# One list-scheduled program in place of phases: tiled attention matmuls with projections and MLP between them

## The chip, the cores and the metric

The kernel runs on one core of one Trainium2 chip. The metric is the time of one execution on the device, in microseconds (us). An execution also has a mean granted TensorE clock, where 1.00 is full speed. In the profile's lines PE is TensorE, PEld its weight loads, ACT ScalarE, DVE VectorE, POOL GpSimd, and PEclk the granted clock. On one core an execution is called slow here when it is over 1.5% longer than the fastest of the same kernel in the same comparison.

## The reference, cut to what matters

A gate mixes a 32-head attention with an MLP. S = 2048 rows, D = 640, head size 20, F = 1536, all in bfloat16.

```python
g = sigmoid((x * gate_w).sum(-1, keepdims=True))
q, k, v = heads(x @ wqkv)                     # 32 heads of 20
a = softmax(q @ k.T * 20**-0.5) @ v @ wo
h = x @ w1 + b1
b = (h * tanh(softplus(h))) @ w2              # Mish
out = g * a + (1 - g) * b
```

Two facts shape everything. A head of 20 fills only 20 of the 128 rows of TensorE in the score product, and 21 of its 128 columns (value plus a column of ones for the denominator) in the value product. And the exponentials are 32 x 2048 x 2048, that is 1.05 million columns of 128 partitions, all on ScalarE.

## The kernel before

First come the projections, the gate and the MLP; then a second block does all attention, then the output projection. In attention a step is one head, one tile of 128 keys and 1024 queries:

```python
def emit_S(s):
    ...
    for c in range(2):                     # KTZ: one head's keys, all other rows zero
        ins = pe.matmul(T[b][:, c * 512:(c + 1) * 512],
                        KTZ[j6][:, kt * P:(kt + 1) * P],     # 128 rows x 128 columns
                        QT[:, g6, q0:q0 + 512], start=True, stop=True)
    ins.then_inc(s_s, 1)

def emit_V(s):
    ...
    for c in range(2):                     # two matmuls on the same column tile
        ins = pe.matmul(OTACC[32 * j:32 * j + DH + 1, c * 512:(c + 1) * 512],
                        V_all[:, kt, h, 0:DH + 1], ETS[b][:, c * 512:(c + 1) * 512],
                        start=(kt == 0), stop=(kt == NKT - 1), tile_position=(0, 32 * j))
    ins.then_inc(s_v, 1)

for s in range(NS):
    emit_V(s)
    if s + ND < NS:
        emit_S(s + ND)
```

ScalarE does one exponential of 1024 columns per step, 1024 in all. No two matmuls share the array.

The softmax here doesn't subtract the row's maximum and nothing guards it: scores larger than these inputs give would overflow.

## Time and profile before

| | before |
|---|---|
| median of three executions | 1542.01 us (1541.35 to 1546.44) |
| projections, gate, MLP | about 365 us, PE 62%, ACT 49% |
| attention | 1109.5 us |
| normalisation of the last group, output projection, stores | about 59 us |
| mean granted clock | 0.955 |

The two lines below, of the page's list of costliest groups, give line, engine, operation, output and inputs, shapes, count, then busy time and mean ns of one, then idle time ahead of it and its releaser.

```profile
L499 ACT ACTIVATE ETS<-T 128x1024 bf16<-128x1024 f32 x1024 | 1048.7, 1024 | 69.3 <-PE T L558 23.8
L558 PE MATMUL T<-QT,KTZ 128*128 128x512 bf16 x2048 | 621.7, 385 | 4.9 <-DMA KTZ<-KT 4.9
```

In a matmul's line, 128\*128 is the part of the array in use, rows by columns. In attention the clock is 1.00 throughout; in the first part it goes down to a half around idle stretches of several us.

### The profile page before, as it was taken

To read this page: it belongs to the slowest core of one execution; us is meant where nothing else is said; L and a number is where in the kernel's file an instruction comes from. 1 tells how busy PE (TensorE), PEld (TensorE's weight loads), DVE (VectorE), ACT (ScalarE), POOL (GpSimd) and SP (SyncE) were. 2 spreads that over 40 slices of the span, in tenths; PEclk is the share of its full clock that TensorE was granted. 3 is DMA by queue.
4 is the path that set the end of the run, shared out by engine and by line. 5 is a ranking of instruction groups with operands and counts; after the bars stand their busy time and mean duration, and the time that the engine had idled before them with its cause. 6 is when DMAs were issued, how large, how long until landed. Compare 5 with 4: busy or idle time off the path is not lost.

```text
span 1541.6 us, 13886 instructions
## 1 busy us (share of the span) xinstructions
PE 1349.1 (88%) x5456; PEld 346.5 (22%) x5456; DVE 235.2 (15%) x200; ACT 1215.1 (79%) x1298; POOL 0.2 (0%) x4
## 2 busy tenths in 40 slices
PE   4665467557999999999999999999999999999958
PEld 2322223222212121121212121221212121121215
DVE  5211110012020202012020202012020202012027
ACT  0334536663999999999999999999999999999940
POOL 0000000000000000000000000000000000000000
PEclk9878779878999999999999999999999999999979
DMA  8000000001010101010110102010110101010011
GB/s 234 0 1 0 0 0 1 0 1 34 5 14 3 14 3 16 1 16 3 14 14 3 7 3 22 1 16 3 14 14 3 14 3 16 1 16 3 5 7 69
DMA packets 23753, 22.79 MB, mean 15 GB/s; under 512 B 14856, under 2 KB 19080, under 8 KB 23688
## 3 DMA queue, kind: packets, MB, share of 16 engines
q1 hardware_dynamic: 20584, 19.44, 9.8%
q10 hardware_dynamic: 3104, 2.46, 0.6%
q8 instruction: 43, 0.70, 0.2%
q14 instruction: 22, 0.18, 0.0%
HBM read 7.21 MB, written 2.62 MB: 6 GB/s over the span
## 4 chain that ended last, share of the span: by engine, by line
PE 73%; DVE 2%; DMA 0%; issue 0%; SPq 0%; ACT 0%; DVEq 0%
PE OTACC L575 35%; PE T L558 35%; PE T L592 2%; DVE OUNG L464 1%; DMA BCSB<-RTMP 0%; PE T L594 0%; DVE RTMP L468 0%; DVE KTZ L449 0%; SPq L538 0%; ACT ETS L499 0%; DVE OTACC L452 0%; DVE OUTT L487 0%; DVE DIFF L482 0%; DVE OTN L472 0%; DVEq L115 0%
## 5 line engine op out<-in xcount | busy, mean ns | idle before, releaser
L499 ACT ACTIVATE ETS<-T 128x1024 bf16<-128x1024 f32 x1024 | 1048.7, 1024 | 69.3 <-PE T L558 23.8
L575 PE MATMUL OTACC<-ETS,V_all 128*21 128x512 bf16 x2048 | 616.8, 383 | 15.1 <-DVE OUNG L464 13.1
L558 PE MATMUL T<-QT,KTZ 128*128 128x512 bf16 x2048 | 621.7, 385 | 4.9 <-DMA KTZ<-KT 4.9
L558 PEld LDWEIGHTS T<-QT,KTZ 128*128 128x128 bf16 x2048 | 116.8, 97 | 445.0 <-ACT ETS L499 429.5
L575 PEld LDWEIGHTS OTACC<-ETS,V_all 128*21 128x21 bf16 x2048 | 106.0, 90 | 451.5 <-issue 426.5
L464 DVE CAST OUNG<-OTACC 128x1024 bf16<-128x1024 f32 x16 | 19.6, 1225 | 834.7 <-PE OTACC L575 834.7
L300 PE MATMUL PB<-XT,WQKV 128*120 128x512 bf16 (+1 forms) x240 | 69.7, 427 | 81.7 <-DVE QT L345 81.7
L468 DVE RECIPROCAL RTMP<-OUNG 128x1024 bf16<-128x1024 bf16 x16 | 104.8, 6553 | 0.6
L316 PE MATMUL PB<-W,ACTT 128*128 128x512 bf16 x192 | 59.5, 408 | 35.0 <-ACT BALL L403 35.0
L394 ACT CAST KT<-PB 120x512 bf16<-120x512 f32 (+1 forms) x24 | 14.0, 585 | 95.6 <-PE PB L300 95.6
L286 PE MATMUL PB<-XT,W 128*128 128x512 bf16 x240 | 65.5, 424 | 11.2 <-ACT UB L370 10.8
L300 PEld LDWEIGHTS PB<-XT,WQKV 128*120 128x120 bf16 (+1 forms) x240 | 31.6, 142 | 116.2 <-DVE QT L345 93.0
L402 ACT CAST BALL<-PB 128x512 bf16<-128x512 f32 x16 | 9.3, 583 | 54.2 <-PE PB L318 54.2
L592 PE MATMUL T<-WOG,OTN 128*128 128x512 bf16 x128 | 36.3, 390 | 17.9 <-DVE OTN L472 17.9
L334 DVE TENSOR_TENSOR ACTT<-HB,UB 128x512 bf16<-128x512 bf16 x48 | 20.4, 425 | 171.9 <-ACT UB L380 168.3
L318 PE MATMUL PB<-W,ACTT 128*128 128x128 bf16 x192 | 44.0, 229 | 0.0
L234 PE MATMUL PB<-WQKV,XT 128*128 128x500 bf16 x80 | 23.7, 394 | 22.4 <-DMA XT<-in_A_x_dram 22.4
L286 PEld LDWEIGHTS PB<-XT,W 128*128 128x128 bf16 x240 | 25.2, 107 | 46.2 <-issue 13.6
L472 DVE TENSOR_TENSOR OTN<-OUNG,BCSB 128x1024 bf16<-128x1024 bf16 x16 | 11.1, 692 | 154.3 <-DMA BCSB<-RTMP 154.3
L316 PEld LDWEIGHTS PB<-W,ACTT 128*128 128x128 bf16 x192 | 19.9, 104 | 64.6 <-ACT BALL L403 38.1
L369 ACT ACTIVATE HB<-PB,B1F 128x512 bf16<-128x512 f32 x48 | 33.6, 700 | 0.7 <-PE PB L286 0.7
L370 ACT ACTIVATE UB<-PB,B1F 128x512 bf16<-128x512 f32 x48 | 33.9, 705 | 0.0
(36 smaller groups left out, 284.0 us busy)
## 6 DMA issues: line engine op xcount, KB each, us to landing
KTZ<-KT SPq DMA_DIRECT2D x64, 80.0 KB
BCSB<-RTMP SPq DMA_DIRECT2D x64, 64.0 KB, 5.9
W<-in_B_w_dram SPq DMA_DIRECT2D x2, 1920.0 KB, 12.9
out_dram<-OUTT SPq DMA_DIRECT2D x16, 160.0 KB, 1.8
WQKV<-in_A_wqkv_dram ACTq DMA_DIRECT2D x1, 2400.0 KB, 9.4
WOG<-in_A_wo_dram SPq DMA_DIRECT2D x4, 200.0 KB
B1T<-in_B_b_dram ACTq DMA_DIRECT2D x12, 0.2 KB, 8.4
XT<-in_A_x_dram SPq DMA_TRANSPOSE x5, 5.1
```

The costliest lines, as they stand in the source:

```text
L286: ins = pe.matmul(hp[:, 0:TCW], W1[:, ft, fc * P:(fc + 1) * P], XT[:, ft, tc * TCW:(tc + 1) * TCW], start=(ft == 0), stop=(ft == NFT - 1))
L300: ins = pe.matmul(QKP[0:mc, 0:512], WQKV[:, ft, c0:c0 + mc], XT[:, ft, qc * 512:(qc + 1) * 512], start=(ft == 0), stop=(ft == NFT - 1))
L316: pe.matmul(BPa[:, 0:512], ACTT[tc % 2][:, fc, tbl * P:(tbl + 1) * P], W2[:, fc, 0:512], start=(fc == 0), stop=(fc == NFC - 1))
L318: ins = pe.matmul(BPb[:, 0:128], ACTT[tc % 2][:, fc, tbl * P:(tbl + 1) * P], W2[:, fc, 512:640], start=(fc == 0), stop=(fc == NFC - 1))
L369: act.activation(HB[b][:, :], hp[:, 0:TCW], AF.Identity, bias=B1F[:, fc:fc + 1], scale=1.0)
L370: act.activation(UB[b][:, :], hp[:, 0:TCW], AF.Exp, bias=B1F[:, fc:fc + 1], scale=1.0).then_inc(s_hp_actdone, 1)
L464: ins = dve.tensor_copy(OUNG[:, :], OTACC[:, :])
L468: ins = dve.reciprocal(RTMP[:, :], OUNG[:, :])
L499: act.activation(ETS[b][:, :], T[b][:, :], AF.Exp, scale=SCALE).then_inc(s_e, 1)
L558: ins = pe.matmul(T[b][:, c * 512:(c + 1) * 512], KTZ[j6][:, kt * P:(kt + 1) * P], QT[:, g6, q0:q0 + 512], start=True, stop=True)
L575: ins = pe.matmul(OTACC[32 * j:32 * j + DH + 1, c * 512:(c + 1) * 512], V_all[:, kt, h, 0:DH + 1], ETS[b][:, c * 512:(c + 1) * 512], start ...
L592: pe.matmul(T[b][:, 0:512], OTN[:, g, atb * P:(atb + 1) * P], WOG[:, g, 0:512], start=(g == 0), stop=(g == NG - 1))
```

## The change

The intent: TensorE paces attention while ScalarE idles through the MLP, so let attention matmuls use several parts of the array at once and put all other matmuls into the time won. A planner runs on the host when the kernel is built. It simulates the five engines with assumed durations, picks the next operation of each engine by priority, and then writes five fixed instruction streams with the semaphores that they need. Below, a chunk is two or three score matmuls, a quad is four value matmuls, and a filler is a matmul of a projection, the MLP or the output projection put between them. The core of the diff:

```diff
+def s_cand(c):                       # a chunk of 3 or 2 units, in turn
+    ...
+        for i in range(n):
+            j = uu % 4
+            bank = (SA if c % 2 == 0 else SB_)[:, i * QW:(i + 1) * QW]
+            r = slice(32 * j, 32 * j + DH)             # row group j, 20 rows
+            ins = h.matmul(bank, KT[r, g, kt * P:(kt + 1) * P], QT[(qc * NG + g) % 3][r, :], start=True, stop=True)
+def v_cand(n):                       # a quad: four heads, four column groups
+    ...
+        for j in range(4):
+            ins = h.matmul(OT[32 * j:32 * j + DH + 1, :], V_all[:, kt, 4 * g + j, :], ETS[:, u % RU, :],
+                           start=(kt == 0), stop=(kt == NKT - 1))
+def e_cand(c):                       # exponentials of 1536 and 1024 columns
+    ...
+        return h.activation(ETS[:, a:a + n, :].rearrange("p u c -> p (u c)"), src, AF.Exp, scale=SCALE)
+def pick_pe():                       # scores first, then values, then a "fill":
+    ...                              # a matmul of a projection, the MLP or the output projection
-                act.activation(UB[b][:, :], hp[:, 0:TCW], AF.Exp, bias=B1F[:, fc:fc + 1],
...                                   # and Ln, Tanh, product
+                return h.activation(a, a, AF.Mish)     # 8 of 3072 columns, in two batches
```

Keys and queries of four heads lie at partitions 0, 32, 64 and 96, each padded by 12 rows of zeros. Evacuations of projections move from ScalarE to VectorE. Normalisation goes through three small transfers per group of four heads. The MLP is in two halves; the hidden layer of a half reuses the memory of weights that are done with.

## The prediction

> **What bounds the kernel now.** I read the strip of 40 slices first. It shows two programs one after the other:
>
> ```profile
> PE   4665467557999999999999999999999999999958
> ACT  0334536663999999999999999999999999999940
> PEclk9878779878999999999999999999999999999979
> ```
>
> Each slice is 38.5 us. For ten slices TensorE and ScalarE are both half busy and the clock is often lowered; then comes a long stretch in which both read 9; then a tail. A table of three stretches gives the sizes (columns: length, then busy time and count of PE, PEld, DVE, ACT, POOL, then granted clock, DMA share, GB/s):
>
> ```profile
> 25.00:365.00 340.00, 210.70 (x1096) 102.20 (x1094) 51.09 (x106) 165.08 (x273) 0.00 (x0) 0.83 0.03 10
> 373.00:1482.50 1109.50, 1096.09 (x4088) 221.94 (x4088) 129.32 (x47) 1045.87 (x1021) 0.00 (x0) 1.00 0.10 9
> 1482.50:1541.60 59.10, 36.98 (x258) 20.29 (x258) 35.81 (x35) 0.00 (x0) 0.00 (x0) 0.86 0.23 49
> ```
>
> So: about 365 us before attention, in which neither engine is full (PE 62%, ACT 49%); 1109.5 us of attention; 59 us of tail. In attention PE and ACT both look full, so the next question is which of them paces the other. The PE timeline of a few steps answers it (start, length, instruction, x how many merged):
>
> ```profile
> 800.09 0.60 PE L575 MATMUL OTACC<-ETS,V_all 128*21 128x512 bf16 x2
> 800.62 0.61 PE L558 MATMUL T<-QT,KTZ 128*128 128x512 bf16 x2
> 801.16 0.60 PE L575 MATMUL OTACC<-ETS,V_all 128*21 128x512 bf16 x2
> ```
>
> A pair of value matmuls and a pair of score matmuls start 0.535 us after each other, so a step is 1.07 us. In the same trace, columns stream at 0.42 ns each at full clock (late output projection: 640 columns each 0.27 us), so 512 columns take 0.216 us and a pair 0.43; about 0.10 us is lost each time PE changes between the two kinds. 4 x 0.216 + 2 x 0.10 = 1.07: PE explains the step alone. ACT's own pace I take from four activations in a row that wait for nobody:
>
> ```profile
> 101.72 2.19 ACT L380 ACTIVATE UB<-UB 128x512 bf16<-128x512 bf16 x4
> L380 ACT ACTIVATE UB<-UB 128x512 bf16<-128x512 bf16 x48 | 26.3, 617 | 0.1
> ```
>
> Each lasts 0.617 us, yet four end in 2.19, so starts are (2.19 - 0.617)/3 = 0.524 apart: consecutive ones overlap by 0.093 us. An exponential of 1024 columns lasts 1.024 us and could therefore start every 0.931 us. It does not:
>
> ```profile
> 796.99 11.72 ACT L499 ACTIVATE ETS<-T 128x1024 bf16<-128x1024 f32 x11
> ```
>
> (11.72 - 1.024)/10 = 1.07 us. **PE paces attention; ACT is 13% faster than it is used.** The chain of waits says the same: 35% of the span each for the two matmul lines, 0.1% for the exponential.
>
> **What the Trainium skill says.** "TensorE: Matmul & The Clock Gate", Part 3, gives for four row tiles of N=512 a measured gain of 3.07, for three column tiles 2.38. No concurrent tiles run in the kernel before: scores multiply a zero-padded 128-row operand, and consecutive value matmuls use the same column tile. So its trace can't confirm this, and the change hangs on it. "TensorEngine Tiling (Array Packing)", Key Properties, says that changing tiling mode drains TensorE; the 0.10 us at every change of kind agrees, though it may be partly the weight load behind the wait. "ScalarE: Activation LUTs", What ACT_TABLE_LOAD costs, gives 0.093 us of overlap between activations, as measured here, and 2.66 us for a change of table set; the load itself is 1.283 us in this trace. "DMA: Bandwidth & Descriptors" puts most of a transfer's fixed 2 us in its completion; the output stores here take 1.8 us from issue to landing.
>
> **The change part by part.**
>
> 1. *Phases merged.* Projections, the MLP and output projection become fillers between attention matmuls. The 365 us in front shrink to a start, and most of the 59 us tail goes.
>
> 2. *Scores on four row groups; values on four column groups.* A score chunk of 3 or 2 tiles goes to different row groups and banks, and a value quad to four column groups. From the gains above: a quad 4 x 0.216/3.07 = 0.28, three tiles 3 x 0.216/2.38 = 0.27, two some 0.25; plus 0.10 for the change of kind: 0.38, 0.37, 0.35 us. These are estimates.
>
> 3. *Exponentials of 1536 and 1024 columns in turn.* 32 heads x 16 key tiles x 4 query blocks = 2048 units of 512 columns; a pair of activations covers five, so 409.6 pairs. At ACT's own pace: 0.931 us for two units; for three, 512 columns more at 0.833 ns, 1.358 us. The pair is 2.289 us, and all of them 938 us. Before, the same columns took 1109.
>
> 4. *PE load beside this.* Each pair needs one chunk of three and one of two (0.72) and 1.25 quads (0.475): 1.20 us. Fillers in all: 560 matmuls of 512 columns (K 160, Q 160, first MLP layer 240) x 0.216 = 121; 640 of 320 columns x 0.135 = 86; 320 V matmuls of 160 columns, no faster than about 0.08 = 26. Sum 233 us, by 410 pairs 0.57. With one extra change per pair 0.1 to 0.2. Total 1.9 to 2.0 of the 2.289 us. **PE goes to some 85% and ACT becomes the bound.** The first quarter is denser: all of K and V, a quarter of Q and part of the first layer, some 80 to 100 us of fillers on 102 pairs, or 0.8 to 1.0 us a pair: with changes 2.2 to 2.4, at the limit.
>
> 5. *Mish in one activation instead of Exp, Ln, Tanh and copies.* The old MLP used 24 table loads. Now two batches of four activations of 3072 columns: 8 x (3072 x 0.833 ns + 0.17) = 22 us, plus four set changes x 2.66 = up to 11, less overlap: about 30 us, all on the ACT path. Evacuations go to DVE: some 200 at 0.5 to 0.7 us, with normalisation about 170 us, far from a bound.
>
> 6. *Start.* Before, PE waited 22.4 us for five 2048-row transposes. Now 512 rows come first (a quarter: issue in some 5 us instead of 18.8, plus 5.1 to land), then K and Q at half clock, 5 x 0.43 us each, and two evacuations: first exponential near 16 us, with some stalls before weights and later rows are in. I charge 24 us.
>
> 7. *Tail after the last exponential.* Quad and copy 1.1, three DMA hops of about 2, 2 and 3 us, reciprocal and multiply 1, eight output projections 64 x 0.135 = 9 us plus 2 for a cold clock, last evacuation and store 3: about 23 us.
>
> 8. *Stalls of ACT.* Dense first quarter about 10; after each Mish batch, in which no score can advance, PE cools and restarts at half clock: 2 x 4; at 32 group ends one accumulator bank is copied out before the next quad may start, about 0.5 each: 16. I charge 35 us.
>
> Sum: 938 + 30 + 24 + 23 + 35 = **1050 us**, 1.47 times faster.
>
> **Rivals.**
>
> *PE stays the bound because tiles do not overlap.* If score and value matmuls ran one after the other, they would need 4096 x 0.216 = 885 us plus changes, 1332 x 0.1 = 133, plus fillers 233: 1250, with start and tail about 1300. For it: PE is the bound today, and no tile runs concurrently in this trace. Against: operands lie at partitions 0, 32, 64, 96, outputs in separate banks or quadrants, issued in succession. Half the effect would put PE at 2.6 to 2.8 us a pair: about 1180.
>
> *The static order jams.* Every queue is fixed by a model with guessed durations (score chunk 0.226, 0.1 per change, a DMA 2.1). Where a DMA of the normalisation lands later than planned, DVE waits at its head with ready evacuations behind it, then PE, and ACT after two chunks. Per group 1 to 2 us would add 30 to 60: 1080 to 1110. For it: five queues in order and 1300 dependent steps. Against: the model's exponential pair is 2.232 us, slightly faster than I expect, so PE, DVE and DMA get a little more time than planned; output stores land in 1.8 us, within the 2.1.
>
> *The clock falls.* Shorter PE work leaves gaps. But in the old first phase the clock dropped around idle stretches of several us (95 to 105: no matmul, clock 0.64) and stood at 0.99 from 200 to 210 with 0.8 us gaps. Gaps here are below 1 us; a low clock doubles PE's work, which fills the gaps and lifts the clock again. Costs some 20 us if wrong.
>
> *Activations do not overlap* behind a semaphore wait: pairs at 1.024 + 1.451 = 2.475 us, 1014 in all, hence 1125 us.
>
> **Range and chances.** Everything as planned, with half the stalls, gives 1010 to 1020. Jams or lost overlap give 1080 to 1125. Range 1010 to 1120. Even without tile concurrency the merged phases save over 2%, so only a badly jammed order or an error I have not seen keeps it from being faster: 0.97 faster, 0.01 the same, 0.02 slower.
>
> **What would show it.** ACT at 9 from the second slice on, and mean exponential starts 2.29 us a pair in the middle; PE at 7 to 9 with score matmuls of a chunk starting together; clock 1.00 there; PE waiting on exponentials and ACT hardly on scores; the chain mostly on ACT; two Mish stretches of 13 to 15 us; first exponential before 20 us; 20 to 25 us after the last. The prediction is wrong if ACT waits for scores by more than some 50 us, if matmuls of one chunk start 0.2 us apart, or if DVE's waits on the broadcast transfers are copied by PE and ACT.

## The result

| | before | changed |
|---|---|---|
| median of all executions | 1543.01 us | 1124.43 us |
| executions | 1541.35 to 1546.44 | 1105.67, 1121.46 (fast), 1127.40, 1158.80 (slow) |
| mean clock of these | 0.955 (profiled) | 0.714, 0.698, 0.695, 0.662 |

The ratio of the fast executions is 0.7218 (0.7164 to 0.7272). Ratios are the mean time of one kernel's fast runs over that of the other's of the same rounds, so not quite the ratio of the medians. The result is correct.

The kernel is much faster, but its times are spread over 5% and are ordered exactly by the clock, which is far below that of before. These are three rows of the strip for the changed kernel, each slice 28 us:

```profile
PE   4999999998799988888999995999889988888785
ACT  2999999999866659999877999779998799999991
PEclk9999999999555575555556996559955555555556
```

For nine slices ACT is full and the clock is full. Then the clock falls to a half and, with two longer returns (72 and 58 us) and a few short ones, stays there; ACT has dips down to 5. A table of three stretches shows what a dip is (columns as in the prediction's table):

```profile
100.00:200.00 100.00, 94.85 (x661) 29.07 (x658) 29.59 (x47) 100.00 (x90) 0.00 (x0) 1.00 0.03 9
300.00:400.00 100.00, 100.00 (x475) 31.76 (x475) 13.03 (x25) 62.77 (x51) 0.00 (x0) 0.55 0.03 11
900.00:1000.00 100.00, 85.43 (x438) 15.71 (x435) 7.68 (x13) 94.92 (x84) 0.00 (x0) 0.50 0.03 9
```

From 100 to 200 us, with full clock, ACT is busy all the time although fillers are dense (661 matmuls). From 300 to 400 us PE is never idle, yet it gets through 475, and ACT through 51 exponentials instead of 90. From 900 to 1000 us there are few fillers, and even at half clock PE nearly keeps up. So a low clock hurts where fillers are dense.

The tiles do run together. This is the timeline at full clock, and after it one at half clock (weight loads and other engines' lines left out, but for one of ACT):

```profile
270.78 0.39 PE L487 MATMUL SA<-QT,KT 20*128 20x512 bf16 x3
271.10 0.40 PE L504 MATMUL OT<-ETS,V_all 128*21 128x512 bf16 x4
271.43 0.39 PE L408 MATMUL MB<-XT,W1F 128*128 128x512 bf16 x1
271.75 0.39 PE L487 MATMUL SB<-QT,KT 20*128 20x512 bf16 x2
```

```profile
331.30 0.61 PE L487 MATMUL SA<-QT,KT 20*128 20x512 bf16 x3
331.84 0.61 PE L504 MATMUL OT<-ETS,V_all 128*21 128x512 bf16 x4
331.95 1.45 ACT L583 ACTIVATE ETS<-SA 128x1536 bf16<-128x1536 f32 x1 [1.24 <-PE SA L487]
332.38 0.45 PE L422 MATMUL MB<-W,WKV 128*128 128x320 bf16 x1
332.76 0.61 PE L487 MATMUL SB<-QT,KT 20*128 20x512 bf16 x2
```

A chunk of three score tiles, a quad of four value tiles and one filler matmul each take 0.32 to 0.33 us from start to start, the change of kind included: three and four tiles cost what one matmul costs. At half clock the chunk and the quad take 0.54 (the filler there is a shorter one, of 320 columns), and ACT waits 1.24 us for the scores.

The groups of the exponentials, and the chain that ended last, of the changed kernel:

```profile
L583 ACT ACTIVATE ETS<-SA 128x1536 bf16<-128x1536 f32 x410 | 642.0, 1566 | 100.4 <-PE SA L487 99.5
L583 ACT ACTIVATE ETS<-SB 128x1024 bf16<-128x1024 f32 x409 | 465.7, 1139 | 16.3 <-PE SB L487 15.4
ACT 62%; PE 35%; DMA 1%; DVE 1%; SPq 1%; issue 0%
```

ACT waits 115 us for scores. The mean lengths, 1566 and 1139 ns, are not costs: one that waits for nobody lasts 1451 and 1024, and in a full queue the record is longer because consecutive ones overlap. Their starts tell the pace: the commonest distance is 1.347 us after an exponential of 1536 columns and 0.904 after one of 1024, 2.25 a pair.

With these, the 1119.7 us of the profiled execution add up. All four parts come from the starts and ends on ACT in the trace: the first exponential starts at 20.3; 410 x 1.347 + 409 x 0.904 = 922; the two Mish batches with their table loads take 13.3 each, 26.6; the last exponential ends 24.6 before the end. What is left, 126 us, is ACT waiting (the 115 us above, and the overlap that is lost at each wait).

### The profile page after: what moved, and what is told of

It reads as the page before. It is cut to its first block, busy times and chain, and to the rows that moved or that the text cites. A ratio compares the mean times of both kernels' runs of the same rounds, so it can differ in the third digit from the quotient of the medians.

```text
span 1119.7 us, 12597 instructions
## 1 busy us (share of the span) xinstructions
PE 981.2 (88%) x5616; PEld 262.8 (23%) x5616; DVE 191.2 (17%) x322; ACT 973.2 (87%) x833; POOL 8.9 (1%) x7
## 4 chain that ended last, share of the span: by engine, by line
ACT 62%; PE 35%; DMA 1%; DVE 1%; SPq 1%; issue 0%
ACT ETS L583 60%; PE MB L422 6%; PE OT L504 6%; PE SA L487 6%; PE MB L432 5%; PE SB L487 5%; PE MB L369 4%; PE MB L408 2%; ACT WKV L593 1%; ACT HHF L593 1%; DMA XT<-in_A_x_dram 1%; SPq L301 1%; PE MB L382 1%; DMA RB<-rdram 0%; DVE OTC L619 0%
## 5 line engine op out<-in xcount | busy, mean ns | idle before, releaser
L583 ACT ACTIVATE ETS<-SA 128x1536 bf16<-128x1536 f32 x410 | 642.0, 1566 | 100.4 <-PE SA L487 99.5
L583 ACT ACTIVATE ETS<-SB 128x1024 bf16<-128x1024 f32 x409 | 465.7, 1139 | 16.3 <-PE SB L487 15.4
L487 PE MATMUL SA<-QT,KT 20*128 20x512 bf16 x1230 | 212.2, 511 | 82.8 <-ACT ETS L583 69.2
L504 PE MATMUL OT<-ETS,V_all 128*21 128x512 bf16 x2048 | 265.2, 510 | 1.8 <-ACT ETS L583 1.0
L487 PE MATMUL SB<-QT,KT 20*128 20x512 bf16 x818 | 210.9, 510 | 15.9 <-ACT ETS L583 13.2
L408 PE MATMUL MB<-XT,W1F 128*128 128x512 bf16 x240 | 82.2, 416 | 0.0
L432 PE MATMUL MB<-WOG,OTN 128*128 128x320 bf16 x256 | 64.5, 395 | 10.0 <-DVE OTN L633 9.8
L369 PE MATMUL MB<-XT,WQP 128*128 128x512 bf16 x160 | 63.6, 483 | 0.0
L422 PE MATMUL MB<-W,WKV 128*128 128x320 bf16 x192 | 54.5, 399 | 9.7 <-ACT HHF L593 9.7
L422 PE MATMUL MB<-W,HHF 128*128 128x320 bf16 x192 | 55.0, 394 | 0.0
L619 DVE COPY OTC<-OT 128x512 f32<-128x512 f32 x32 | 22.1, 692 | 188.5 <-PE OT L504 188.4
L372 DVE CAST QT<-MB 128x512 bf16<-128x512 f32 x32 | 22.1, 691 | 147.9 <-PE MB L369 147.9
L633 DVE TENSOR_TENSOR OTN<-OTC,RB 128x512 bf16<-128x512 f32 x32 | 22.1, 691 | 105.4 <-DMA RB<-rdram 105.3
L432 PEld LDWEIGHTS MB<-WOG,OTN 128*128 128x128 bf16 x256 | 27.4, 117 | 43.5 <-issue 17.6
L385 DVE CAST KT<-MB 128x512 bf16<-128x512 f32 x32 | 22.1, 691 | 54.6 <-PE MB L382 54.6
L422 PEld LDWEIGHTS MB<-W,WKV 128*128 128x128 bf16 x192 | 19.4, 114 | 39.0 <-issue 19.2
```

Source lines behind the costliest of these rows:

```text
L369: return h.matmul(b[:, :], WQP[:, i, g * P:(g + 1) * P], XT[:, i, qc * 512:(qc + 1) * 512], start=(i == 0), stop=(i == NFT - 1))
L372: NFT, 216.0, lambda h, b: h.tensor_copy(QT[gi % 3][:, :], b[:, :]),
L385: lambda h, b: h.tensor_copy(KT[:, g, tc * 512:(tc + 1) * 512], b[:, :]), 600.0, [], ("K", g, tc))
L408: return h.matmul(b[:, :], W1[:, i, fc * P:(fc + 1) * P], XT[:, i, tc * 512:(tc + 1) * 512], start=(i == 0), stop=(i == NFT - 1))
L422: return h.matmul(b[:, 0:320], hslice(i, tl * P, P), W2[:, i, hh * 320:(hh + 1) * 320], start=(i == 0), stop=(i == NFC - 1))
L432: return h.matmul(b[:, 0:320], OTN[:, i, tl * P:(tl + 1) * P], WOG[:, i, hh * 320:(hh + 1) * 320], start=(i == 0), stop=(i == NG - 1))
```

## The experiments

The theory after the result: those 126 us are the low clock, which makes PE the bound in dense stretches. The rival: the fixed order jams, whatever the clock. All kernels but one (said there) give the right result.

### Throwaway matmuls in the gaps

```diff
+        if (True) and (slack is None or slack > 330) and (fills or active or stt["v"] < NQ):
+            for b in range(2):               # a projection bank that nobody uses now
+                ...
+                c = Cand(need, 216.0, lambda h, b=b: h.matmul(MB[b][:, 0:512], XT[:, 0, 0:P], XT[:, 0, 0:512], start=True, stop=True), None, mode="F")
```

The next user of the bank starts its accumulation anew, so the result is not touched. 601 such matmuls go in.

> Adds throwaway matmuls of 512 columns into a free projection bank wherever the plan leaves TensorE idle for more than 0.33 us, nothing else. Theory (half clock): the changed kernel lost about 126 us of ScalarE stalls because the granted clock was 0.5 for some 670 us and the dense filler stretches then became TensorE-bound. Then the clock stays at 1.00 nearly throughout (mean above 0.97), ScalarE stalls outside Mish fall below 30 us, and the time is 1000 to 1030 us. Rival (the fixed order jams whatever the clock): stalls stay near 126 us or grow, and the time is 1110 to 1180 us.

Measured: 1039.67 us at clock 0.969 in the one fast execution; 1073.87, 1101.83 and 1102.67 at 0.925, 0.893 and 0.885 in slow ones. Half right, and the time missed the range. Its strip (the profiled execution, a slow one) shows why:

```profile
ACT  2999999999966639999999997776699999999991
PEclk9999999999855589999999996555599999999999
```

Twice the clock is still lost, just after each Mish batch, for 99 and 136 us, and just there ACT dips. Everywhere else, where the changed kernel had a half clock, it is full, and ACT nearly so (94.5 of the 100 us from 400 to 500). So the clock can be held in sparse stretches by giving the array work, but once lost it was not won back here for some 100 us of dense work.

The control has the same throwaway matmuls at the same places, 64 columns wide instead of 512:

> Control for e3_warm: the same throwaway matmuls at the same places in the order, planned with the same duration, but of 64 columns, so that the array streams little. Theory (the clock follows the streaming of the array): the clock still falls, mean below 0.8, time 1090 to 1160 us. Rival (any instruction at all keeps the clock, or it is the changed order that helped): as e3_warm, 1000 to 1030 us.

Measured: 1137.79 us at 0.688 (fast) and 1158.87 at 0.667 (slow). That is no better than the changed kernel, and its strip has the half clock again:

```profile
PEclk9999999999555755555559985555555555555556
```

Its real matmuls stand in exactly the order of the run before (310 of 5616 at another place than in the changed kernel). The changed order and the extra instructions bring nothing; the streaming does.

### Score tiles of 32 rows instead of 20

```diff
-                r = slice(32 * j, 32 * j + DH)
+                r = slice(32 * j, 32 * j + 32)
```

The 12 further rows hold zeros already, so the result is the same, and so is the length of a matmul.

> Score matmuls contract over all 32 rows of their row group (the 12 extra rows are zeros) instead of 20. Time for the array is the same. If the clock control counts rows or cells in use, mean clock rises above 0.80 and the time falls to about 1050 us; if it counts time in which the array streams, clock stays at 0.66 to 0.72 and time at 1105 to 1160 us, which I expect.

I expected no effect, and was wrong. Measured: 1050.12 and 1054.06 us, both fast, at clock 0.793 and 0.783; ratio to before 0.6812 (0.6791 to 0.6834).

```profile
ACT  1999999999999689999989999999997999999990
PEclk9999999999989965655689995999755855555556
300.00:350.00 50.00, 48.44 (x359) 17.72 (x356) 8.40 (x16) 50.00 (x46) 0.00 (x0) 1.00 0.05 15
```

At the first Mish batch the half clock lasts 13.7 us instead of 109.2 in the changed kernel (from the traces' clock records; from TensorE's restart after the batch it is 7.8 us instead of 103), and ACT is busy for all of the 50 us from 300 to 350, where in the changed kernel it is the bottom of the dip. Only the number of array rows in use changed; the order of the matmuls is the same to the last one. So with these two kernels the granted clock, 0.793 and 0.783 against 0.714 to 0.662, depended on how many rows work, and not only on whether a matmul is in flight.

### No tiles together

```diff
-                r = slice(32 * j, 32 * j + DH)
+                r = slice(0, DH)
-                ins = h.matmul(OT[32 * j:32 * j + DH + 1, :], V_all[:, kt, 4 * g + j, :], ETS[:, u % RU, :],
-                               start=(kt == 0), stop=(kt == NKT - 1))
+                ins = h.matmul(OT[0:DH + 1, :], V_all[:, kt, 4 * g + j, :], ETS[:, u % RU, :],
+                               start=True, stop=True)
```

> Wrong result on purpose: all score matmuls use row group 0 and all value matmuls column group 0 (without accumulation), so that no two tiles can run together; everything else is unchanged. If concurrent tiles carry the gain: TensorE streams 885 us of attention plus 233 us of fillers plus changes of kind, is never idle, the clock stays near 1.00, and the time is 1200 to 1330 us. If the merged order alone carried it, the time stays at 1105 to 1160 us.

Its output is wrong, which doesn't matter for the time. Measured: 1582.46 us (fast) and 1649.12 us (slow), slower than the kernel before. The stretches of 100 to 300 and 500 to 560 us, both at full clock:

```profile
100.00:300.00 200.00, 199.84 (x887) 60.29 (x886) 37.23 (x61) 140.47 (x116) 0.00 (x0) 1.00 0.02 7
500.00:560.00 60.00, 59.79 (x300) 23.75 (x299) 12.66 (x23) 33.08 (x27) 0.00 (x0) 1.00 0.05 16
```

PE is full, and 116 exponentials are done in 200 us instead of the 180 of the changed kernel's stretch of the same clock. So with this order, merging and planning alone are worth nothing: concurrent tiles carry the gain. From start to start a chunk of three and a quad take 0.74 and 0.97 us here instead of 0.32 and 0.33:

```profile
560.01 0.82 PE L487 MATMUL SA<-QT,KT 20*128 20x512 bf16 x3
560.75 1.03 PE L504 MATMUL OT<-ETS,V_all 128*21 128x512 bf16 x4
561.72 0.60 PE L487 MATMUL SB<-QT,KT 20*128 20x512 bf16 x2
```

The expectation was too low by 250 us, and the clock is part of it: in this run TensorE has a matmul in flight for 97% of the span, and still the mean clock is 0.84. At 563 us it fell though PE had not paused for more than 0.20 us in the 100 us before. That a matmul is in flight is thus not enough, as in the run of 32 rows. But the share of the array in use does not explain both runs: the same matmuls spread over 1582 instead of 1121 us fill less of the array on average, and yet the mean clock is higher, 0.84 against 0.70. What exactly is counted stays open.

### Both remedies together, and only part of one

On another chip, with the changed kernel once more beside them:

> The changed kernel itself once more, so that it stands on the same chip as the next two. If its spread comes from the clock, each execution's time falls with its mean clock: about 1105 us at 0.71 and 1160 us at 0.66, as before.

Measured: 1133.56 and 1133.74 us (fast) at 0.685 and 0.689; 1153.23 and 1155.03 (slow) at 0.665 and 0.666. The 1105 us did not come again, and time falls with the clock as before.

> Both earlier edits together: scores contract over 32 rows (12 of zeros), and throwaway matmuls fill planned gaps of TensorE. Theory (the clock is the whole loss, and it follows how much of the array is in use): clock above 0.95, ScalarE stalls outside Mish below 20 us, 995 to 1020 us in every execution. If something else costs the 80 us that the 32-row run still lost to waiting and Mish, it stays at 1040 us or more.

Measured: 1017.12, 1017.34, 1020.12 and 1024.44 us, all fast, at 0.998, 0.998, 0.995 and 0.988. The ratio to before is 0.6615 (0.6594 to 0.6635). The strip and the chain:

```profile
ACT  1999999999999949999999999999999999999990
PEclk9999999999999999999999999999999999999999
ACT 90%; PE 8%; DMA 1%; SPq 1%; DVE 0%; issue 0%
```

ACT is full from the second slice to the last but one, but for one slice that is looked at below, and the spread between executions is 0.7% instead of 1.9% on that chip and 4.8% on the first. ACT's waits outside Mish fall from 126 to about 21 us, with the order of real matmuls that brought the 64-column control nothing. The low clock is thus shown to be the cause of about 105 us of waiting (126 less 21; the two profiled executions are on different chips, and the changed kernel's on the second chip waits a little longer, 137 us).

> 32 rows, and throwaway matmuls only while ScalarE runs Mish. If the pause of the scores during Mish starts the low clock and the rest follows, it is as good as the run with throwaway matmuls everywhere, 995 to 1020 us. If sparse attention stretches lower the clock by themselves, it stays near the 32-row run, 1030 to 1055 us, which I expect.

Measured: 1043.61 and 1045.90 us, both fast, at 0.799 and 0.797. As I expected, the Mish pauses are not the whole: now the clock holds through the first Mish batch but falls at 372 us, in a stretch with few fillers. The throwaway matmuls between sparse attention matmuls are worth the other 26 us.

### The one jam that remains

In the run with both remedies one wait of ACT stands out:

```profile
368.98 1.02 ACT L590 ACTIVATE ETS<-SB 128x1024 bf16<-128x1024 f32 x1 [13.00 <-PE SB L487]
```

In the 13 us ahead of it PE works through the second MLP layer and the output projection (lines L422 and L432), then a query projection, then the scores that need it. It is in the changed kernel too, 13.52 us near 404 us. I put query projections 24 quads earlier in the plan:

```diff
-        fills.append(Fill("Q", (qc, g), gi * 16, gi * 16 - 24, ...
+        fills.append(Fill("Q", (qc, g), gi * 16 - 24, gi * 16 - 24, ...
```

> The run with 32 rows and throwaway matmuls, and the query projections due 24 quads earlier in the plan, so that they go ahead of the second MLP layer and the output projection. That run still had one wait of ScalarE of 13.0 us at 355 to 369 us, in which TensorE worked through projections that the plan had put ahead of a query projection that the next scores needed. If the plan's priority is the cause, the wait goes and the time is 1003 to 1010 us; if the wait comes from the output stores that happen there, it stays at 1015 to 1025 us.

Measured, with both remedies: 1015.27 to 1022.05 us, median 1018.20, all fast, ratio 0.6598 (0.6583 to 0.6613). That is no gain over the 1018.73 without it. The wait became shorter but did not go (7.19 us), and the second Mish batch, where the clock was lost for 27 us in this execution, took back as much. What else holds that query projection up, I have not settled.

> The changed kernel with the earlier query projections alone, 20 rows and no throwaway matmuls. The 13.5 us wait near 390 us should go, but the clock is still low for most of the time: 1090 to 1150 us at a mean clock of 0.65 to 0.72. If the jam in the plan, not the clock, were the main loss, the time would fall below 1080 us.

Measured, on the changed kernel alone: 1087.51 us (fast) at clock 0.734, and 1116.75, 1130.26 and 1186.11 (slow) at 0.703, 0.690 and 0.640. The time is not below 1080, and again it follows the clock. But the range was missed on both sides. The one fast execution is 46 us faster than the fast ones of the changed kernel on this chip, at a higher clock, and the slowest is 31 us slower than the slowest there; whether the new order helps the clock, these four do not show. A jam of 13 us exists; it is not the main loss.

## Why the prediction was right or wrong

It was right in direction and about size, and the two fast executions average 1113.6 us, inside the range near its upper end. But the median of all four, 1124.43, lies just outside, and on the second chip all four executions do. The middle, 1050 us, was missed by 64 us, and one term explains that:

| term | predicted | changed, profiled | with both remedies, profiled |
|---|---|---|---|
| before the first exponential | 24 | 20.3 | 22.1 |
| exponentials | 938 | 922 | 922 |
| Mish | 30 | 26.6 | 26.6 |
| other waits of ACT | 35 | 126 | 21 |
| after the last exponential | 23 | 24.6 | 23.5 |
| sum | 1050 | 1119.5 | 1015.2 |

**The bound before.** Right. Once the scores no longer share PE's time with padded rows, ACT took its own pace, even a little faster than predicted: 2.25 us a pair where the prediction had 2.289, because consecutive exponentials overlap by 0.10 to 0.12 us (1.451 long and 1.347 apart; 1.024 long and 0.904 apart) and not by 0.093.

**Tiles.** The mechanism was right, and the serial run shows that it carries the gain. The estimate of 0.35 to 0.38 us for a chunk or a quad was above the measured 0.32 to 0.33. It had taken the page's gains crosswise, that of four row tiles for the quad of column tiles and that of three column tiles for the row tiles.

**ACT becomes the bound at 85% of PE.** Right at full clock (100 to 200 us, ACT 100%), even in the dense first quarter, where the prediction feared 10 us of waits and the trace has under 4 in the first 250 us.

**Stalls, 35 us.** This is the term that failed, 126 us in its place, and inside it the step on the clock. The prediction saw the rival "the clock falls", and dismissed it with: "Gaps here are below 1 us; a low clock doubles PE's work, which fills the gaps and lifts the clock again. Costs some 20 us if wrong." The first half holds, the 9.7 us pause of TensorE at the first Mish batch apart: at half clock the gaps did fill, PE was busy for 100.00 of 100 us. The second half does not: the clock stayed at a half for 109.2 us. One of the prediction's own signs of being wrong came true, too: ACT waited for scores by 115 us, where it allowed some 50. That the fast executions still fell inside the range is partly luck, since its upper part was meant for jams or lost overlap. The prediction looked at idle time only, since in the kernel before a low clock had always come with idle stretches; but all score matmuls of that kernel used the whole array, 128\*128. The change that made attention cheap also took away work that held the clock: with 32 instead of 20 rows its mean rose from about 0.70 to 0.79. Its share was sized at 4 us after each Mish batch and measured at about 105 us in all.

**Start, Mish, tail.** Within 4 us each. Mish was where the clock went first, as expected, but the recovery was not: the half clock lasted 109 and 72 us for an assumed 4.

**The rival of a jammed order.** Present with one wait of 13 us, for which a wrong priority was blamed and only partly confirmed; not the 1 to 2 us in each of 32 groups that the prediction described.

## What to carry to other kernels

When matmuls shrink to tiles, check the granted clock in stretches, not only busy time: a TensorE that looks 100% busy can be at half speed and stay there, as it did here. If rows of a row group are free, give them zeros and use them all; if an engine that is not the bound has gaps, throwaway matmuls of full width can hold its clock. Together they made this kernel 1018.7 us instead of 1106 to 1159, and steady.

## What the Trainium skill lacked or had wrong

- "TensorE: Matmul & The Clock Gate", Part 1, has the full clock return after one busy window of about 3.4 us. Here it stayed at a half for 109.2 us, in the last 103 of which TensorE had no gap above 0.56 us (44.4 us in all in the run with earlier query projections alone). With 32 instead of 20 rows in use per score tile, in the same order, it returned after 13.7 us, 7.8 of them after the pause for Mish. It also names idle gaps of more than about 3.4 us as what loses the clock; with one small tile at a time it was lost, at 563 us of the serial run, without such a gap. The page says nothing on how much of the array has to work; where the thresholds lie, and whether columns count as rows do, these runs leave open.
- The same page, Part 3, measures 3.07 for four row tiles and 2.38 for three column tiles. Here three row tiles and four column tiles each took as long as one full matmul, 0.32 and 0.33 us from start to start, against 0.74 and 0.97 one at a time: 2.3 and 2.9 times with the change of kind counted in, and by estimate close to 3 and 4 without it, if the 0.10 us of the kernel before is taken off all four.
- "ScalarE: Activation LUTs" has back-to-back activations overlap by about 93 ns. That held for four activations of 512 columns from SBUF in the kernel before; the exponentials out of PSUM overlapped by 104 to 120 ns.
